# Sparse attention and mixture of experts on one core: q, k and v laid out beforehand, loaded into the tiles' own order

## The chip, the cores and the metric

The kernel runs on one core of one Trainium2 chip. The metric is the device time of one launch in microseconds, the median of several runs. A profile is one execution recorded by the hardware profiler; its span runs from the first to the last instruction. The arrays that a launch gets are prepared on the host by numpy; that is outside the time, in both kernels.

## The reference

Attention over q, k, v of shape (8 batches, 8 heads, 576 positions, 64), float32. Heads 0 to 3 see the last 32 positions (local), heads 4 to 7 the positions with the same remainder by 32 (strided). Its output, reshaped to 4608 tokens of 512, goes through a mixture of 8 experts, two for each token.

```python
scores = scale * np.matmul(q, k.transpose(0, 1, 3, 2))          # scale = 1/8
mask_local = (rel >= 0) & (rel < 32)                            # rel = pos[:, None] - pos[None, :]
mask_strided = (rel >= 0) & (pos[None, :] % 32 == pos[:, None] % 32)
scores = np.where(masks[None], scores, -1e9)
attn = np.exp(scores - scores.max(-1, keepdims=True))
attn = attn / (attn.sum(-1, keepdims=True) + 1e-09)
out = np.matmul(attn, v)
# then, for each token x of 512: the two best of 8 experts by x @ w_gate + softplus(x @ w_noise) * noise
out[token] += weight * (np.maximum(x @ w1[e], 0) @ w2[e])
```

## The kernel before

The work is written as pieces (`Piece`), each with an engine, an assumed duration, what it reads and writes, and a rank. A planner (`issue_all`, L296) walks through them with a clock of its own and writes them out in the order in which each engine could take them; pieces marked ANY go to ACT or DVE, whichever is free first. Buffers are rings (`Ring`): a piece that allocates the n-th slot waits for the users of the slot before it. When the planner sees PE waiting for an attention piece, it puts matmuls of zeros into the gap (L375, padding, one for each 150 ns that it reckons). Loads and stores are issued by SP, in order, on one queue; GpSimd issues the scatters and gathers, in order too. Zero stores to the output (12 of 0.79 MB) have the lowest rank and are taken when the planner's queue is nearly empty.

**Attention.** A unit is one batch, one pair of heads, local or strided: 32 units, four to a batch, strided first. For each unit:

- `loads` (L447): k and q as rows of positions (ks, qs or raw), v into v_s by way of vraw, or straight into v_l in pieces of 64 numbers, and v_0, the first 64 rows again.
- `prep` (L494): k and q are turned by PE, four groups of transposes a unit (L519 strided, four to a group; L515 local, three to a group, after a reordering copy into ord). ACT or DVE evacuates each group into kT or qT (q times the scale). For strided heads eight more small copies fill the ninth block. kT and qT have one buffer of each kind.
- `products` (L541): masks (L560) and scores (L567) into two PSUM banks, five blocks in each.
- `item` (L580), twice a unit, i = 0 and 1: maxima (L594), exps (L598, L600), transposes of the weights (L608) and their copies (aT), the value matmuls (L627, L632), row sums, reciprocals and scaling (L637 to L657) into xo. The value tiles hold a column of ones, so that the row sums come out of the same matmuls. The item with i = 1 has a fifth, extra block, whose two heads lie in the 64 lower partitions side by side in columns (`extra`).
- `finish` (L666): xo goes to x_dram by SP (L673), and is transposed for the gate (L694, L698).

After four units `route` (L723) runs the gate matmuls (L744) and, on ACT and DVE, picks two experts for each token; GpSimd scatters the entries into the experts' lists (L834). So there are eight gates, one a batch.

**Experts.** Six lists can be started before all batches are known: two are known after batches 2 and 3, the others later. Layer 1 is L1062, layer 2 is L1114; the weights are loaded in 160 pieces (wraw) and split in two parts by ACT and DVE (L904, L905). Results (res, a ring of four) are scatter-added to the output by GpSimd (L1150), after the zero stores of those rows.

Of the kernel before, what the change touches and what calls it, by code (L numbers as in the profile page):

```python
# [22 lines left out]
def kernel(  # L23
    ctx: ExitStack,
    tc: tile.TileContext,
    q: bass.AP,
    k: bass.AP,
    v: bass.AP,
# [8 lines left out]
    B, H, S, D = q.shape  # L37
# [5 lines left out]
    NP = HL // 2  # L43
    QB = 64
# [7 lines left out]
    LP, LJ = S // 6, 6  # L52
# [105 lines left out]
    kT_l = keep.tile([128, STRIDE + S], F32, name="kT_l")  # L158
    qT_l = keep.tile([128, NBL, QB], F32, name="qT_l")
    kT_s = keep.tile([128, NBL, G], F32, name="kT_s")  # L160
    qT_s = keep.tile([128, NBL, G], F32, name="qT_s")
    v_l = [keep.tile([KW, 2, NBL, D + 1], F32, name=f"v_l{i}") for i in range(2)]
    v_s = [keep.tile([G, 2, NJ, D + 1], F32, name=f"v_s{i}") for i in range(2)]

    v_0 = [keep.tile([G, 2, D + 1], F32, name=f"v_0{i}") for i in range(2)]
    xo_ = [keep.tile([128, 5, 2, D], F32, name=f"xo{i}") for i in range(3)]
    nc.vector.memset(kT_l[:, :STRIDE], 0.0)
    for i in range(2):
        nc.vector.memset(v_l[i][:, :, :, D:D + 1], 1.0)
        nc.vector.memset(v_l[i][:STRIDE, 0, 0, :], 0.0)  # L170
        nc.vector.memset(v_0[i][QB:], 0.0)
        nc.vector.memset(v_0[i][:QB, :, D:D + 1], 1.0)
        nc.vector.memset(v_s[i][:, :, :, D:D + 1], 1.0)
    nc.vector.memset(kT_s[:, NBL - 1, QB:], 0.0)
    for x in xo_:
        nc.vector.memset(x[QB:, 4, :, :], 0.0)
# [264 lines left out]
    R["v_l"], R["v_s"], R["v_0"] = Ring(2, fixed=v_l), Ring(2, fixed=v_s), Ring(2, fixed=v_0)  # L441

    def base_of(u):
        b, p, local = units[u]
        return (b * H + (2 * p if local else HL + 2 * p)) * S * D

    def loads(u, rank):  # L447

        base, local = base_of(u), units[u][2]
        res = {}  # L450

# [846 lines left out]
```

## Time and profile before

| what | us |
|---|---|
| median of 3 runs (1105.77 to 1109.4) | 1107.29 |
| the profiled execution | 1117.46 |
| its span | 1115.7 |
| fourth gate, where the first expert list follows | 151 |
| eighth and last gate | 366 |

The page gives each engine's busy time: PE runs matmuls, PEld loads their weights beside them, DVE and ACT are the vector engines, POOL is GpSimd, SP issues DMAs. The chain of work is followed back from the last instruction, at each step to what released it. A row `L515 x3` in the chain means three instructions of line 515 in a row, with the time that they held the chain. In rows by line, `145/161/164` are the shortest, median and longest duration in ns.

### The profile page before, as it was taken

The page shows a single profiled execution, that of the slowest core. Times are in us where ns is not written, and L with a number is a line of the kernel's source. Part 1 is how long each engine was busy: PE and PEld are TensorE (multiplying, and loading weights), DVE is VectorE, ACT ScalarE, POOL GpSimd, SP SyncE. Part 2 cuts the span into 40 slices and gives each one's busy share as a digit, 9 for nine tenths or more (in the row PEclk, how much of TensorE's full clock was granted, in tenths as well). Part 3 has the DMA queues.
Part 4 walks back from the last instruction along what each step waited for, and adds up shares of the span by engine and source line. Part 5 has one row for each costly group of instructions (what it writes and reads, how often), then busy time and mean ns, then how long its engine had stood idle before and what let it go on. Part 6 is the DMA issues. An engine that isn't in the chain of part 4 may idle for free.

```text
span 1115.7 us, 23537 instructions
## 1 busy us (share of the span) xinstructions
PE 1069.2 (96%) x8790; PEld 945.9 (85%) x8790; DVE 556.0 (50%) x1536; ACT 474.3 (43%) x1203; POOL 539.8 (48%) x661
## 2 busy tenths in 40 slices
PE   8988887989999999999999999999999999999997
PEld 7867766888788898988879898989989898989886
DVE  7857766865476224624746236323633462355231
ACT  6867766766565222423433224222512252244221
POOL 1044334423424467655668475646554655556432
PEclk9998989989999999999999999999999999999999
DMA  9986857878785134543555235523642363243222
GB/s 199 241 195 153 221 137 207 193 179 208 181 245 136 29 52 97 137 75 72 141 133 133 43 57 136 115 44 54 163 85 46 59 179 61 44 116 81 43 46 31
DMA packets 168430, 133.03 MB, mean 119 GB/s; under 512 B 51864, under 2 KB 136344, under 8 KB 168296
## 3 DMA queue, kind: packets, MB, share of 16 engines
q1 hardware_dynamic: 145160, 92.31, 32.1%
q0 software_dynamic: 23136, 38.94, 19.9%
q8 instruction: 83, 1.36, 0.5%
q14 instruction: 51, 0.42, 0.1%
HBM read 92.85 MB, written 39.39 MB: 119 GB/s over the span
## 4 chain that ended last, share of the span: by engine, by line
PE 87%; issue 5%; DVE 3%; DMA 1%; ACT 1%; POOL 1%; another core or an unknown queue 1%; POOLq 0%; SPq 0%; DVEq 0%; ACTq 0%
PE bankB L1114 6%; PE bankE L1114 5%; PE bankF L1114 5%; PE bankC L1062 5%; PE bankH L1062 5%; PE bankG L1062 5%; PE bankE L1062 5%; PE bankC L1114 5%; PE bankF L1062 4%; PE bankD L1062 4%; PE bankA L1062 4%; PE bankA L1114 4%; PE bankB L1062 4%; PE bankG L1114 4%; PE bankH L1114 3%
## 5 line engine op out<-in xcount | busy, mean ns | idle before, releaser
L985 POOL DMA_INDIRECT xg<-x_dram,gxx x248 | 258.5, 1043 | 165.8 <-DVE xr L1024 71.8
L1150 POOL DMA_INDIRECT out_dram<-res,tabt x80 | 133.4, 1667 | 99.7 <-ACT res L289 54.0
L834 POOL DMA_INDIRECT tab<-ent,addr x96 | 91.3, 951 | 89.9 <-issue 26.8
L1024 DVE STREAM_TRANSPOSE xr<-xg 128x512 f32<-128x512 f32 (+1 forms) x66 | 68.1, 1032 | 42.4 <-DMA xg<-x_dram,gxx 33.8
L1031 ACT CAST xhi<-xr 128x512 fp32r<-128x512 f32 (+1 forms) x66 | 39.1, 592 | 53.1 <-DVE xr L1024 51.2
L1033 DVE TENSOR_TENSOR xlo<-xr,xhi 128x512 fp32r<-128x512 f32 (+1 forms) x66 | 43.5, 659 | 35.9 <-ACT xhi L1031 25.2
L905 DVE TENSOR_TENSOR w1lo<-wraw,w1hi 128x512 fp32r<-128x512 f32 x80 | 54.5, 686 | 3.7 <-ACT w1hi L904 1.3
L905 DVE TENSOR_TENSOR w2lo<-wraw,w2hi 128x512 fp32r<-128x512 f32 x80 | 51.8, 684 | 1.2 <-ACT xT L288 0.7
L994 POOL TENSOR_SCALAR gix<-tabt 128x2 int32<-128x2 int32 (+1 forms) x32 | 8.0, 251 | 88.2 <-DMA tabt<-tab 71.0
L904 ACT CAST w1hi<-wraw 128x512 fp32r<-128x512 f32 x80 | 49.0, 618 | 0.4 <-DMA wraw<-in_moe_w_dram 0.2
L904 ACT CAST w2hi<-wraw 128x512 fp32r<-128x512 f32 x80 | 46.6, 617 | 3.3 <-DMA wraw<-in_moe_w_dram 2.7
L1062 PE MATMUL bankH<-xhi,w1hi 128*128 128x256 f32 (+3 forms) x132 | 40.5, 307 | 0.8 <-issue 0.8
L1062 PE MATMUL bankG<-xhi,w1hi 128*128 128x256 f32 (+3 forms) x132 | 40.0, 303 | 0.6 <-issue 0.6
L1062 PE MATMUL bankG<-xlo,w1hi 128*128 128x256 f32 (+3 forms) x132 | 39.4, 299 | 1.0 <-issue 1.0
L1062 PE MATMUL bankC<-xhi,w1hi 128*128 128x256 f32 (+3 forms) x132 | 39.8, 301 | 0.0
L1062 PE MATMUL bankH<-xhi,w1lo 128*128 128x256 f32 (+3 forms) x132 | 39.6, 300 | 0.0
L1062 PE MATMUL bankH<-xlo,w1hi 128*128 128x256 f32 (+3 forms) x132 | 39.6, 300 | 0.0
L1062 PE MATMUL bankG<-xhi,w1lo 128*128 128x256 f32 (+3 forms) x132 | 39.4, 298 | 0.0
L1062 PE MATMUL bankC<-xlo,w1hi 128*128 128x256 f32 (+3 forms) x132 | 39.1, 296 | 0.1
L1062 PE MATMUL bankC<-xhi,w1lo 128*128 128x256 f32 (+3 forms) x132 | 39.2, 297 | 0.0
L1114 PE MATMUL bankB<-w2hi,hhi 128*128 128x512 f32 x96 | 38.9, 405 | 0.0
L1062 PE MATMUL bankF<-xhi,w1hi 128*128 128x256 f32 (+3 forms) x128 | 38.2, 299 | 0.4 <-issue 0.4
(696 smaller groups left out, 3545.8 us busy)
## 6 DMA issues: line engine op xcount, KB each, us to landing
wraw<-in_moe_w_dram SPq DMA_DIRECT2D x160, 256.0 KB
out_dram<-zeros SPq DMA_DIRECT2D x12, 768.0 KB
ks<-in_k_dram SPq DMA_DIRECT2D x15, 320.0 KB
qs<-in_q_dram SPq DMA_DIRECT2D x15, 320.0 KB
vraw<-in_v_dram SPq DMA_DIRECT2D x30, 160.0 KB
raw<-in_k_dram SPq DMA_DIRECT2D x16, 288.0 KB
v_l<-in_v_dram SPq DMA_DIRECT2D x16, 288.0 KB
raw<-in_q_dram SPq DMA_DIRECT2D x16, 288.0 KB
```

The lines of the kernel that those rows point to most:

```text
L834: st = nc.gpsimd.indirect_dma_start(out=tab, out_offset=bass.IndirectOffsetOnAxis(ap=s["addr"].t[:, t, kk:kk + 1], axis=0), in_=s["ent"].t ...
L904: Piece("ACT", 620, lambda o: nc.scalar.copy(hi.t, raw.t), rank, read=[raw], alloc=[hi], expert=True)
L905: Piece("DVE", 715, lambda o: nc.vector.tensor_tensor(lo.t, raw.t, hi.t.bitcast(F32), ALU.subtract), rank, read=[raw, hi], alloc=[lo], exp ...
L985: dma(lambda o, g=g: nc.gpsimd.indirect_dma_start(out=xg.t[:, g, :], out_offset=None, in_=x_dram[:4 * known, :], in_offset=bass.IndirectOf ...
L994: nc.gpsimd.tensor_scalar(gi.t[:, :nb], tb.t[:, :nb, 0], known - 1, None, op0=ALU.min)
L1024: Piece("DVE", 8.8 * rows, lambda o, xg=xg, xr=xr, ng=ng, rows=rows: nc.vector.transpose(xr.t.rearrange("p (c x) -> p c x", c=ND)[:, :, :r ...
L1031: Piece("ACT", 620 * rows // 128, lambda o, view=view, cols=cols: nc.scalar.copy(xh.t[:, :, cols], view()), rank, read=[xr], expert=True, ...
L1033: Piece("DVE", 725 * rows // 128, lambda o, view=view, cols=cols: nc.vector.tensor_tensor(xl.t[:, :, cols], view(), xh.t[:, :, cols].bitca ...
L1062: nc.tensor.matmul(ps.t[:, :width], a.t[:, 128 * d:128 * d + 128], c.t[:, d, :width], start=(m == 0), stop=(m == len(todo) - 1))
L1114: nc.tensor.matmul(ps.t, HT[n, f][p[0]].t[:, cols], W2[n][f][p[1]].t, start=(m == 0), stop=(m == len(todo) - 1))
L1150: st = nc.gpsimd.indirect_dma_start(out=out[:known, :], out_offset=bass.IndirectOffsetOnAxis(ap=places(), axis=0), in_=y.t[:rows, :], in_o ...
```

## The change

The host turns q and k of each unit and stacks the two heads, so that a load fills kT and qT in place, 128 rows of 2304 or 2560 bytes. v is laid out with its column of ones; rows are 4680 bytes, and the strided tile holds the ninth block (the first 64 rows again) too. `prep` is gone with its transposes, evacuations and copies, and so are raw, ord, ks, qs, vraw and v_0. kT and qT get two buffers of each kind; mx goes from 3 to 5, ex and aT from 2 to 3, rs from 2 to 4 buffers, res from 4 to 3. q is no longer scaled: a tensor_scalar multiplies the maximum by the scale, and the exps apply it to the scores. The two heads of the extra block now lie one above the other in 128 partitions: one sum and one reciprocal cover all five blocks, and two copies with a factor, on ACT or DVE, take the extra blocks to xo in place of one product on DVE.

```diff
     R = {}
     for name, shape, dtype, depth in (
-            ("raw", [LP, 2, LJ, D], F32, 2), ("ord", [LP, LJ, 2, D], F32, 1),
-            ("vraw", [GP, NJ, D], F32, 1), ("ks", [GP, 2, NJ, D], F32, 1), ("qs", [GP, 2, NJ, D], F32, 1),
-            ("mx", [128, 5], F32, 3), ("ex", [128, 5, KW], F32, 2), ("aT", [128, 5, 128], F32, 2),
-            ("rs", [128, 6], F32, 2),
+            ("mx", [128, 5], F32, 5), ("ex", [128, 5, KW], F32, 3), ("aT", [128, 5, 128], F32, 3),
+            ("rs", [128, 6], F32, 4),
...
-    R["kT_l"], R["qT_l"] = Ring(1, fixed=[kT_l]), Ring(1, fixed=[qT_l])
-    R["kT_s"], R["qT_s"] = Ring(1, fixed=[kT_s]), Ring(1, fixed=[qT_s])
+    R["kT_l"], R["qT_l"] = Ring(2, fixed=kT_l), Ring(2, fixed=qT_l)
+    R["kT_s"], R["qT_s"] = Ring(2, fixed=kT_s), Ring(2, fixed=qT_s)
...
+        def put(key, ring, sel, src, rows, width, rank):
+            slot = res[key] = R[ring].new()
+            dma(lambda o: nc.sync.dma_start(sel(slot.t), dram(src, n * rows * width, [[width, rows], [1, width]])),
+                4 * rows * width, rank, alloc=[slot])
...
+            put("k", "kT_l", lambda t: t[:, STRIDE:], k_l, 128, S, rank)
+            put("q", "qT_l", lambda t: t.rearrange("r n x -> r (n x)"), q_l, 128, S, rank)
+            put("v", "v_l", lambda t: t[STRIDE:].rearrange("p h n d -> p (h n d)"), v_l, QB, VW, v_rank)
...
+            put("k", "kT_s", lambda t: t.rearrange("r n x -> r (n x)")[:, :8 * G + QB], k_s, 128, 8 * G + QB, rank)
+            put("q", "qT_s", lambda t: t.rearrange("r n x -> r (n x)"), q_s, 128, S, rank)
+            put("v", "v_s", lambda t: t.rearrange("p h n d -> p (h n d)"), v_s, GP, VW, v_rank)
         return res
-
-    def prep(u, L, rank):
...
+        Piece("DVE", 90, lambda o: nc.vector.tensor_scalar(mx.t, mx.t, scale, None, op0=ALU.mult), rank, write=[mx],
+              read=[mx])
+
         def exps(o):
             for n in range(4):
-                nc.scalar.activation(exv()[:, n, :], view(sc)[:, n, :], AF.Exp, bias=mx.t[:, n:n + 1])
+                nc.scalar.activation(exv()[:, n, :], view(sc)[:, n, :], AF.Exp, bias=mx.t[:, n:n + 1], scale=scale)
...
-                    rhs = L["v"].t[:, h, NBL - 1, :] if local else L["v0"].t[:, h, :]
-                    nc.tensor.matmul(extra()[:, h, :], aT.t[:w, 4, 64 * h:64 * h + 64], rhs, start=True, stop=True)
+                    rhs = L["v"].t[:w, h, NBL - 1, :]
+                    nc.tensor.matmul(main(5)[64 * h:64 * h + 64, 4, :], aT.t[:w, 4, 64 * h:64 * h + 64], rhs, start=True,
+                                     stop=True)
...
-            nc.vector.tensor_scalar(rs.t[:, :4], main()[:, :, D], 1e-9, None, op0=ALU.add)
-            if nb > 4:
-                nc.vector.tensor_scalar(rs.t[:QB, 4:], extra()[:, :, D], 1e-9, None, op0=ALU.add)
+            nc.vector.tensor_scalar(rs.t[:, :nb], main(nb)[:, :, D], 1e-9, None, op0=ALU.add)
...
-            if nb > 4:
-                nc.vector.tensor_tensor(xo.t[:QB, 4, :, :], extra()[:, :, :D],
-                                        rs.t[:QB, 4:, None].to_broadcast([QB, 2, D]), ALU.mult)
...
+        for h, r in enumerate(halves) if nb > 4 else ():
+            Piece("ANY", {"ACT": 270, "DVE": dve(D)}, lambda o, h=h, r=r: copy(
+                o.e, xo.t[:QB, 4, h, :], main(5)[r, 4, :D], rs.t[r, 4:5]), rank, read=[po, rs], write=[xo])
...
-            ("res", [128, DM], F32, 4)):
+            ("res", [128, DM], F32, 3)):
...
+def _laid_out(q, k, v):
...
+    def turned(a):
+        return a.transpose(0, 1, 2, 4, 3).reshape(B, NP, 2 * D, -1)
...
+    vl = np.ones((B, NP, QB, 2, NB, D + 1), v.dtype)
+    vl[..., :D] = pairs(v, 0).reshape(B, NP, 2, NB, QB, D).transpose(0, 1, 4, 2, 3, 5)
...
+    return {"q_l": turned(pairs(q, 0)), "k_l": turned(pairs(k, 0)), "v_l": vl,
+            "q_s": strided(q, G - QB), "k_s": strided(k, 0), "v_s": vs}
```

Because the planner sets the order, it moves as a whole. Three places matter.

PE at the start of the program, behind the warm-up (zeros), before: the four groups that turn k and q of the first strided unit, then its masks.

```order
L337 MATMUL bankH<-zeros 128x256
L519 MATMUL bankA<-ident,ks 128x72 x4
L519 MATMUL bankB<-ident,ks 128x72 x4
L519 MATMUL bankC<-ident,qs 128x72 x4
L519 MATMUL bankD<-ident,qs 128x72 x4
L560 LDWEIGHTS twin
L560 MATMUL bankE<-mask_s,twin 64x288
```

PE at the same place after the change:

```order
L331 MATMUL bankH<-zeros 128x256
L481 LDWEIGHTS twin
L481 MATMUL bankA<-mask_s,twin 64x288
L481 LDWEIGHTS twin
L481 MATMUL bankA<-mask_s,twin 64x72
```

The masks follow the warm-up at once. Over the whole program 448 transposes in 128 groups are gone, and the padding of zeros grows from 137 to 210 matmuls.

PE behind the fourth gate, where the first expert list begins, before: scores of the next local unit (L567), then a matmul of zeros (L1069) and layer 1 (L1062).

```order
L567 MATMUL bankB<-kT_l,qT_l 64x96
L567 MATMUL bankD<-kT_l,qT_l 64x96
L1069 LDWEIGHTS zeros
L1069 MATMUL bankE<-zeros 128x256
L1062 MATMUL bankE<-xhi,w1hi 128x256
```

And after, where padding is L369, values are L547 and L552, transposed weights L531, layer 1 L977:

```order
L369 LDWEIGHTS zeros
L369 MATMUL bankE<-zeros 128x256
L547 MATMUL bankE<-vt_s_147,aT 64x65 x8
L552 MATMUL bankE<-vt_s_147,aT 64x65 x2
L531 MATMUL bankB<-ident,ex 96x128 x4
L984 LDWEIGHTS zeros
L984 MATMUL bankC<-zeros 128x256
L977 MATMUL bankC<-xhi,w1hi 128x256
```

The first list moves further into the fifth batch. Ahead of the last gate stand 216 layer-1 and 120 layer-2 matmuls, where there were 372 and 168.

SP at the end of batch 2, before: the first zero store (L1199) stands between stores of xo (L673) and loads (L455).

```order
L455 DMA vraw<-in_v_dram 80x512
L673 DMA x_dram<-xo_147 128x2x128
L673 DMA x_dram<-xo_147 64x128
L1199 DMA out_dram<-zeros 1536x1x128
L455 DMA raw<-in_q_dram 96x2x384
L455 DMA v_l_140<-in_v_dram 64x18x64
```

SP after the change, around the last store of batch 7 (the rows of xo_148), where the first zero stores (L1114) now are:

```order
L1114 DMA out_dram<-zeros 1536x1x128
L443 DMA vt_l_145<-in_v_l_dram 64x1170
L1114 DMA out_dram<-zeros 1536x1x128
L588 DMA x_dram<-xo_148 128x4x128
L588 DMA x_dram<-xo_148 64x128
L1114 DMA out_dram<-zeros 1536x1x128 x2
L588 DMA x_dram<-xo_149 128x2x128 x2
```

All twelve zero stores move behind the loads of batch 7; SP issues 96 loads of q, k and v in place of 128.

More of the change, by code (lines that the diff above doesn't have):

```diff
@@ L25 @@
     tc: tile.TileContext,
-    q: bass.AP,
-    k: bass.AP,
-    v: bass.AP,
+    q_l: bass.AP,
+    k_l: bass.AP,
+    v_l: bass.AP,
+    q_s: bass.AP,
+    k_s: bass.AP,
+    v_s: bass.AP,
     w_gate: bass.AP,
@@ L156 @@
     psum = actx.enter_context(tc.tile_pool(name="psum", bufs=1, space=PSUM))
[L158 to L165, printed above, removed]
+    kT_l = [keep.tile([128, STRIDE + S], F32, name=f"kT_l{i}") for i in range(2)]
+    qT_l = [keep.tile([128, NBL, QB], F32, name=f"qT_l{i}") for i in range(2)]
+    kT_s = [keep.tile([128, NBL, G], F32, name=f"kT_s{i}") for i in range(2)]
+    qT_s = [keep.tile([128, NBL, QB], F32, name=f"qT_s{i}") for i in range(2)]
+    vt_l = [keep.tile([KW, 2, NBL, D + 1], F32, name=f"vt_l{i}") for i in range(2)]
+    vt_s = [keep.tile([GP, 2, NBL, D + 1], F32, name=f"vt_s{i}") for i in range(2)]
     xo_ = [keep.tile([128, 5, 2, D], F32, name=f"xo{i}") for i in range(3)]
-    nc.vector.memset(kT_l[:, :STRIDE], 0.0)
     for i in range(2):
[L169 to L176, printed above, removed]
+        nc.vector.memset(kT_l[i][:, :STRIDE], 0.0)
+        nc.vector.memset(kT_s[i][:, NBL - 1, QB:], 0.0)
+        nc.vector.memset(vt_l[i][:STRIDE, 0, 0, :], 0.0)
     nc.vector.memset(run, 0.0)
@@ L444, in base_of, with loads @@
+    def loads(u, rank, v_rank=None):
         b, p, local = units[u]
[L445 to L450, printed above, removed]
[L452 to L468 removed]
@@ L476, in front @@
             def front(o):
-                vv = slot.t.rearrange("p h n d -> p (h n) d")
-                copy(o.e, vv[:STRIDE, 1:, :D], vv[QB:, :2 * NBL - 1, :D])
-            Piece("ANY", {"ACT": act(64 * (2 * NBL - 1)), "DVE": 760}, front, rank, read=[slot], write=[slot])
-        else:
-            slot = res["v"] = R["v_s"].new()
-            for h in range(2):
-                put(f"v{h}raw", R["vraw"].new(), [(lambda t: t[:rows].rearrange("p j d -> p (j d)"), v, base + h * S * D,
-                                                   [[NJ * D, rows], [1, NJ * D]], 2048 * rows)], True)
-                def spread(o, h=h, raw=res[f"v{h}raw"]):
-                    copy(o.e, slot.t[:G, h, :, :D], raw.t[:G])
-                Piece("ANY", {"ACT": act(NJ * D), "DVE": 420}, spread, rank, read=[res[f"v{h}raw"]],
-                      **{"write" if h else "alloc": [slot]})
-            put("v0", R["v_0"].new(),
-                [(lambda t: t[:QB, :, :D], v, base, [[D, QB], [S * D, 2], [1, D]], 65536)], True)
@@ new lines, in front @@
+                vv = slot.t.rearrange("p h n d -> p (h n d)")
+                copy(o.e, vv[:STRIDE, D + 1:], vv[QB:, :VW - D - 1])
+            Piece("ANY", {"ACT": act(VW - D - 1), "DVE": 760}, front, rank, read=[slot], write=[slot])
+        else:
+            put("k", "kT_s", lambda t: t.rearrange("r n x -> r (n x)")[:, :8 * G + QB], k_s, 128, 8 * G + QB, rank)
+            put("q", "qT_s", lambda t: t.rearrange("r n x -> r (n x)"), q_s, 128, S, rank)
+            put("v", "v_s", lambda t: t.rearrange("p h n d -> p (h n d)"), v_s, GP, VW, v_rank)
@@ L565, in product @@
                 rhs = kT.t[r, QB * blk:QB * blk + KW] if local else kT.t[r, blk, :]
-                q0 = 0 if local or blk == NBL - 1 else G0
-                nc.tensor.matmul(sv[b][halves[half], s, :], qT.t[r, blk, q0:q0 + QB], rhs, start=False,
+                nc.tensor.matmul(sv[b][halves[half], s, :], qT.t[r, blk, :], rhs, start=False,
                                  stop=True, skip_group_check=True)
@@ L1286 @@
     arrays, args = {}, []
-    for name in _INS:
-        a = _np.ascontiguousarray(inputs[name])
+    given = _laid_out(inputs["q"], inputs["k"], inputs["v"])
+    given.update((name, inputs[name]) for name in _INS)
+    for name in given:
+        a = _np.ascontiguousarray(given[name])
         arrays[f"in_{name}_dram"] = a
```

117 lines of the change are left out of this document (35 added, 82 removed).

## The prediction

> **What bounds the kernel now.** I read the page first, for the engines and for the chain of work that ended last.
>
> ```profile
> span 1115.7 us, 23537 instructions
> PE 1069.2 (96%) x8790; PEld 945.9 (85%) x8790; DVE 556.0 (50%) x1536; ACT 474.3 (43%) x1203; POOL 539.8 (48%) x661
> PE 87%; issue 5%; DVE 3%; DMA 1%; ACT 1%; POOL 1%; another core or an unknown queue 1%; POOLq 0%; SPq 0%; DVEq 0%; ACTq 0%
> ```
>
> TensorE (PE) is busy for 96% of the span and carries 87% of the chain. That is an average over stages, so I then cut the span at the gate matmuls. The timeline shows them for the fourth and for the last batch:
>
> ```profile
> 151.25 2.78 PE L744 MATMUL bankF<-xT,wg 128*32 128x192 f32 x24
> ...
> 365.60 1.50 PE L744 MATMUL bankD<-xT,wg 128*32 128x192 f32 x24
> ```
>
> The busy time by stretch, from two answers of the same view (columns: stretch, length, PE, PEld, DVE, ACT, POOL, granted clock, DMA share, GB/s):
>
> ```profile
> 0.00:152.00 152.00, 132.94 (x2092) 108.61 (x2095) 109.92 (x449) 109.11 (x350) 44.42 (x113) 0.97 0.84 196
> 25.00:50.00 25.00, 24.60 (x454) 20.93 (x453) 21.43 (x78) 21.95 (x79) 0.00 (x0) 1.00 0.93 234
> ...
> 152.00:366.00 214.00, 200.18 (x2321) 172.35 (x2318) 136.54 (x488) 136.25 (x384) 79.15 (x131) 0.97 0.74 186
> ```
> ```profile
> 79.00:114.00 35.00, 31.41 (x466) 26.18 (x463) 25.31 (x108) 27.07 (x89) 12.51 (x27) 0.90 0.75 166
> ...
> 366.00:1116.00 750.00, 736.08 (x4389) 664.91 (x4383) 309.53 (x599) 228.94 (x471) 416.22 (x418) 0.99 0.40 85
> ```
>
> There are three stages. To 152 us there is attention alone: PE, DVE, ACT and the DMA engines are all well filled (87%, 72%, 72%, 84%), and part of what PE does there is padding. From 152 to 366 us attention and the first expert lists share PE, which idles 13.8 of 214 us. After 366 us the experts alone keep PE busy for 736 of 750 us, and nothing there is edited. So what the change brings is how much earlier the last gate comes, corrected for expert work that moves across it.
>
> **What the change removes.** The transposes of q and k (L515, L519), first to 152 us, then to 366 us, and the padding matmuls (L375), which all lie before 152 us:
>
> ```profile
> 0.00:152.00 152.00, 15.72 (x108) 10.61 (x108) 0.97 0.84 196
> 152.00:366.00 214.00, 11.96 (x84) 9.37 (x84) 0.97 0.74 186
> ```
> ```profile
> 0.00:152.00 152.00, 15.15 (x152) 13.08 (x152) 0.97 0.84 196
> 152.00:366.00 214.00, 10.40 (x104) 9.16 (x104) 0.97 0.74 186
> ```
> ```profile
> 0.00:152.00 152.00, 20.21 (x137) 13.28 (x137) 0.97 0.84 196
> ```
>
> Their busy time, 53.2 us, overlaps other matmuls. What a group holds PE for is seen in the chain (start, length):
>
> ```profile
> 22.25 0.47 PE bankA L515 x3
> 22.71 0.25 PE bankC L515 x3
> ...
> 25.14 0.25 PE bankB L519 x4
> ...
> 27.68 0.11 PE bankG L375
> ```
>
> 0.25 us a group packed, up to 0.47 us with its wait. On ACT and DVE go the evacuations, the reordering copies (ord) and the spreads (v_s). By tile over the whole run, columns PE, PEld, DVE, ACT; the PE figures are mostly other work:
>
> ```profile
> 0.00:1116.00 1116.00, 17.71 (x576) 13.93 (x576) 10.89 (x40) 16.66 (x57) 0.99 0.53 119
> ```
> ```profile
> 0.00:1116.00 1116.00, 17.71 (x576) 13.93 (x576) 11.51 (x43) 16.21 (x53) 0.99 0.53 119
> ```
> ```profile
> 0.00:1116.00 1116.00, 19.29 (x576) 17.91 (x576) 6.92 (x16) 7.84 (x17) 0.99 0.53 119
> ```
> ```profile
> 0.00:1116.00 1116.00, 19.29 (x576) 17.91 (x576) 8.21 (x18) 6.69 (x14) 0.99 0.53 119
> ```
> ```profile
> 0.00:1116.00 1116.00, 27.67 (x192) 19.98 (x192) 5.48 (x10) 18.29 (x22) 0.99 0.53 119
> ```
> ```profile
> 0.00:1116.00 1116.00, 24.06 (x512) 19.32 (x512) 6.84 (x18) 9.86 (x16) 0.99 0.53 119
> ```
>
> These are kT_s, qT_s, kT_l, qT_l, ord and v_s: 49.9 us on DVE and 75.6 us on ACT, 125 of the 492 us that the two do before 366 us. They bound nothing by themselves there (64 to 72% busy), so I book no time of their own for them; they let PE's waits shrink.
>
> **What it adds.** The extra blocks' own sums, reciprocal and scaling go; two copies of 64x64 and a scaling of mx (128x5) come. Nearest rows:
>
> ```profile
> L639 DVE TENSOR_SCALAR rs<-bankG x7: 141/142/145, 24.2 to 345.2; 64x2 f32<-64x2 f32 x7
> ```
> ```profile
> L644 DVE RECIPROCAL rs<-rs x32: 124/126/128, 18.3 to 359.1; 64x2 f32<-64x2 f32 x32
> ```
> ```profile
> L656 DVE TENSOR_TENSOR xo<-bankG,rs x7: 268/273/273, 24.9 to 345.8; 64x128 f32<-64x128 f32 x7
> ```
> ```profile
> L288 ACT COPY xT<-bankA x5: 212/212/234, 43.2 to 218.4; 128x64 f32<-128x64 f32 x5
> ```
>
> Gone: 32 x (142 + 126 + 273) = 17.3 us of DVE. New: 64 x 0.21 = 13.4 us on either engine, and 64 scalings that no row shows: between 0.06 us (half of L644, the smallest DVE row here) and 0.14 us (L639), 4 to 9 us; I take 0.13. All of it is covered by the 125 us removed. The scaling also stands between the maximum and the exps; three ex and five mx buffers cover that, and without the cover it is 64 x 0.13 = 8 us. The scale inside the exps is free: the same 320 instructions. Two of the new copies in place of one product change nothing on PE, which has the same 64 extra value matmuls.
>
> Padding rises from 137 to 210 matmuls, 73 x 0.11 = 8 us. It fills waits of PE and costs nothing as long as they last; if they are gone, 8 us. That the order holds more of it says that PE is expected to wait, not to be full, before the first list.
>
> res has three buffers for four. The next block comes 5.4 us later (second row below); a scatter takes 1.67 us behind its write, so three slots last 16 us. Cost nothing in the last stage.
>
> ```profile
> L1150 POOL DMA_INDIRECT out_dram<-res,tabt x80 | 133.4, 1667 | 99.7 <-ACT res L289 54.0
> ```
> ```profile
> 464.35 2.10 PE bankB L1062 x12
> ...
> 530.35 5.45 PE bankE L1114 x24
> ```
>
> The zero stores move behind batch 7's stores. The first scatter to the output needs three of them (2.4 MB, 12 us at 196 GB/s); on GpSimd batch 7's table scatters queue behind it, and on ACT the fourth res write and the exps behind that. If SP is late, up to 12 us; I take none, since PE holds four unfinished lists there.
>
> **The sum, first stage.** PE without the transposes and the padding would need 132.9 - 15.7 - 15.2 - 20.2 = 82 us; DVE and ACT about 75 us each (219 less 58% of 121, the share of the transposes that falls here). The DMA engines need more: counted from SP's order, 27.4 MB are issued up to the fourth batch's last store (28.9 before), and with the 1 MB of other traffic that the run had on top (29.8 MB at 196 GB/s), 28.4 MB. At the 234 GB/s of 25 to 50 us that is 121 us, at the stage's 196 GB/s 145 us. The loads now have two sets of buffers and no step behind them, so the queue is filled more evenly; I take the middle, 215 GB/s: 132 us, a gain of 20 (7 to 31).
>
> One row bears on the wide rows that the change brings (256-byte packets of v are gone). From 12 to 18 us most packets were small ones:
>
> ```profile
> DMA packets 2375, 1.36 MB, mean 226 GB/s; under 512 B 1782, under 2 KB 2153, under 8 KB 2373
> ```
>
> 226 GB/s, 3% under the best stretch, so I book nothing for packet size. The Trainium skill (DMA: Bandwidth & Descriptors, Specifications) has it that a transfer needs 512 bytes to run at line rate. By that rule the 5.8 MB of v in such pieces (16 x 0.29 and 16 x 0.066, 10 of 16 loads in this stage) cost about double, an estimate of 17 us more gain in this stage and 11 in the next, a sum of 1041 us; this row does not bear it out.
>
> **Second stage.** 84/3 + 104/4 = 54 groups go. Packed they are 54 x 0.25 = 13.5 us, by busy time 22.4; I take 18, since the chain shows both kinds. DMA needs 33 MB in it, 177 us at 186 GB/s, and 214 - 18 - 34 (below) = 162 us asks for 204 GB/s, between the two rates.
>
> **Expert work that moves.** By the order, 216 instead of 372 layer-1 and 120 instead of 168 layer-2 matmuls stand before the last gate. 84 of the former are 384 wide (2.10 us for 12), 72 are 256 wide, two thirds of that, 48 are L1114: 14.7 + 8.4 + 10.9 = 34 us less before the gate and 34 more behind it, where PE is full. Net 0. So the last gate should come at 366 - 20 - 18 - 34 = 294 us, and 784 us should follow.
>
> The profiled execution took 1117.5 us (span 1115.7); the sum is -20 - 18 = -38 us. The runs without profile have their median at 1107.3, 10 us lower, and the same work in them, so I forecast **1069 us**; its own range is 1053 (both terms at their best) to 1085 (-10 and -13).
>
> **Rivals.**
> *The DMA engines keep their pace.* If loads, not copies, set the rate, stage one takes 28.4 MB / 196 = 145 us (-7) and stage two 33 / 186 = 177, against 180 without it (-3): 1097 us. For it: share 0.84, and 0.93 while PE was fullest. Against: ACT and DVE rows stand between load and product today. Chance 0.15.
> *All waits go.* 234 GB/s throughout (-31), and stage two loses its 22 us of transposes and its 14 us idle: -67, 1040 us. Against: four engines with hand-overs have never been that tight here. 0.14.
> *Wide rows move slower (slower).* v now comes in 64 or 80 rows of 4680 bytes, few pieces for 16 engines, and products wait for whole tiles. Both stages hold 28.4 + 33 = 61.4 MB; the last gate must come by 332 us (366 - 34) to break even, so it decides at 185 GB/s, hardly below the 190 of today. At 170 GB/s the gate comes at 361 us, +29: 1136 us. For it, a v_l load on the chain:
>
> ```profile
> 8.87 8.71 DMA v_l<-in_v_dram
> ```
>
> 8.7 us for 0.29 MB, but beside other loads. Against: every filled stretch above ran at 196 GB/s or more. 0.08.
> *PE's clock falls.* With more waiting the granted clock of stage one could drop; it was 0.90 in 79 to 114 us with PE 90% busy. At half clock PE's 82 us become 164: +12, less 18, 1101 us. The Trainium skill (TensorE: Matmul & The Clock Gate, HAM oscillation) states that idle gaps over some 3.4 us halve the clock; that speaks against taking work off a waiting PE, and the padding is there to meet it. 0.05.
> That the change does not do what it says is out: the order has no q or k transposes left.
>
> **How the numbers follow.** 0.58 for the forecast, 0.15 + 0.14 + 0.08 + 0.05 for the rivals. The range runs from 1042 (most of the way to "all waits go") to 1097 (the DMA pace) and leaves out slower and the tail, under 0.2. This kernel's runs tell 0.3%, 3.3 us, from no change. Faster: 0.58 + 0.15 + 0.14 and part of the clock's case, 0.89; same 0.03; slower 0.08.
>
> **What would show it.** After: no transposes of q and k; the fourth gate near 132 us and the last near 294; DMA over 200 GB/s to there; PE full behind it with 784 us to go; mx scaling near 0.13 us. The forecast is wrong if the last gate comes after 320 us, if PE waits for loads at 196 GB/s or less, if ACT waits at a res write around batch 7, or if PE idles more than 20 us after the last gate.

## The result, and the profile after

| | before | after | ratio, 95% interval |
|---|---|---|---|
| first set of runs, median (us) | 1106.53 (1105.01 to 1109.4, 4 runs) | 1079.1 (1073.75 to 1082.25, 4 runs) | 0.974 (0.970 to 0.979) |
| the profiled executions (us) | 1117.46 | 1080.45 | |
| a later set on another chip, median (us) | 1110.07 (1105.52 to 1114.21, 7 runs) | 1073.69 (1069.96 to 1079.05, 4 runs) | 0.969 (0.963 to 0.974) |

The kernel became faster by 27 us in the first set and by 36 us in the second. The forecast was 1069 us with a range of 1042 to 1097. Against the profiled execution, on which the sum was made, the difference is 37 us, for 38 in the sum.

The page of the kernel after, first lines and the chain:

```profile
span 1078.2 us, 22402 instructions
PE 1043.4 (97%) x8415; PEld 916.9 (85%) x8415; DVE 516.0 (48%) x1373; ACT 424.1 (39%) x1069; POOL 538.2 (50%) x661
PE 90%; issue 5%; DMA 1%; DVE 1%; ACT 1%; POOL 1%; SPq 0%; POOLq 0%; another core or an unknown queue 0%; DVEq 0%; ACTq 0%
```

PE lost 26 us of busy time, DVE 40 and ACT 50. The fourth and the last gate in the timeline (start, length):

```profile
133.65 1.50 PE L659 MATMUL bankE<-xT,wg 128*32 128x192 f32 x24
...
295.03 1.50 PE L659 MATMUL bankH<-xT,wg 128*32 128x192 f32 x24
```

They stood at 151.25 and 365.60; 132 and 294 were forecast. The three stages, in the columns of before (stretch, length, PE, PEld, DVE, ACT, POOL, clock, DMA share, GB/s):

```profile
0.00:134.00 134.00, 119.41 (x1903) 93.51 (x1906) 85.96 (x357) 86.10 (x279) 43.59 (x109) 0.94 0.79 211
134.00:295.00 161.00, 154.00 (x1910) 125.22 (x1901) 101.43 (x387) 92.44 (x288) 64.53 (x123) 0.96 0.75 194
295.00:1079.00 784.00, 769.99 (x4609) 698.16 (x4608) 328.64 (x632) 245.54 (x503) 430.08 (x431) 0.99 0.44 94
```

DVE and ACT are now busy for 64% of the first stage, not 72%; the last stage is as full as before. The last gate came 71 us earlier, but expert work was moved across it. Expert matmuls that still stand before it, layer 1 (L977) and layer 2 (L1029):

```profile
0.00:295.00 295.00, 37.10 (x216) 32.24 (x216) 0.95 0.77 202
```
```profile
0.00:295.00 295.00, 34.01 (x120) 21.99 (x120) 0.95 0.77 202
```

That is 71.1 us, for 63.89 + 45.97 = 109.9 before. **Last gate less the expert work ahead of it** takes that move out: 365.6 - 109.9 = 255.7 us before, 295.0 - 71.1 = 223.9 us after. I call it the attention's time; it fell by 32 us. It still counts TensorE's waits, and expert matmuls fill some of them, so it compares only kernels with much expert work ahead of the last gate. One run below has hardly any (6.5 us), and there it says little. For every run, each with its own rows read in the same way:

| kernel | ratio to before (95%) | fourth gate | last gate | expert PE ahead | attention's time |
|---|---|---|---|---|---|
| before | | 151.3 | 365.6 | 109.9 | 255.7 |
| before, again | 1.005 (1.002 to 1.009) | 152.4 | 366.7 | 111.9 | 254.8 |
| after | 0.974 (0.970 to 0.979) | 133.7 | 295.0 | 71.1 | 223.9 |
| after, again | 0.969 (0.963 to 0.974) | 131.2 | 290.5 | 68.9 | 221.6 |
| after, no padding | 0.976 (0.972 to 0.980) | 140.0 | 299.2 | 70.5 | 228.7 |
| after, half the loads | 0.968 (0.964 to 0.973) | 131.0 | 294.0 | 70.4 | 223.5 |
| after, both of these | 0.975 (0.970 to 0.979) | 136.0 | 295.2 | 69.0 | 226.2 |
| after, single tiles | 0.980 (0.975 to 0.985) | 153.2 | 345.0 | 105.9 | 239.1 |
| after, transposes back | 0.987 (0.983 to 0.991) | 139.3 | 308.7 | 69.1 | 239.6 |
| after, copies back | 1.014 (1.009 to 1.019) | 151.3 | 316.6 | 61.9 | 254.6 |
| after, copies planned | 1.006 (1.004 to 1.008) | 140.5 | 273.8 | 6.5 | 267.3 |
| after, v in pieces | 0.973 (0.968 to 0.978) | 136.0 | 295.3 | 68.5 | 226.8 |
| after, no scaling of mx | 0.962 (0.960 to 0.964) | 133.0 | 293.4 | 71.3 | 222.1 |
| before, deeper | 1.003 (0.999 to 1.006) | 143.9 | 338.8 | 85.0 | 253.7 |

Two profiles of one kernel agree in it within 2.3 us.

### The profile page after: what moved, and what is told of

Read it like the earlier page. It is cut to its first block, busy times and chain, and to the rows that moved or that the text cites. A ratio compares the mean times of both kernels' runs of the same rounds, so it can differ in the third digit from the quotient of the medians.

```text
span 1078.2 us, 22402 instructions
## 1 busy us (share of the span) xinstructions
PE 1043.4 (97%) x8415; PEld 916.9 (85%) x8415; DVE 516.0 (48%) x1373; ACT 424.1 (39%) x1069; POOL 538.2 (50%) x661
## 4 chain that ended last, share of the span: by engine, by line
PE 90%; issue 5%; DMA 1%; DVE 1%; ACT 1%; POOL 1%; SPq 0%; POOLq 0%; another core or an unknown queue 0%; DVEq 0%; ACTq 0%
PE bankB L1029 5%; PE bankE L1029 5%; PE bankD L1029 5%; PE bankC L977 5%; PE bankH L977 5%; PE bankF L977 5%; PE bankC L1029 5%; PE bankB L977 5%; PE bankA L977 4%; PE bankE L977 4%; PE bankG L977 4%; PE bankA L1029 4%; PE bankF L1029 4%; PE bankD L977 4%; PE bankH L1029 4%
## 5 line engine op out<-in xcount | busy, mean ns | idle before, releaser
L1065 POOL DMA_INDIRECT out_dram<-res,tabt x80 | 130.7, 1634 | 85.9 <-ACT res L283 53.8
L749 POOL DMA_INDIRECT tab<-ent,addr x96 | 93.8, 977 | 90.7 <-issue 17.5
L977 PE MATMUL bankC<-xhi,w1lo 128*128 128x256 f32 (+3 forms) x136 | 40.3, 296 | 1.0 <-issue 1.0
L977 PE MATMUL bankC<-xhi,w1hi 128*128 128x256 f32 (+3 forms) x136 | 40.8, 300 | 0.2 <-issue 0.2
L977 PE MATMUL bankC<-xlo,w1hi 128*128 128x256 f32 (+3 forms) x136 | 40.3, 297 | 0.5 <-issue 0.5
L977 PE MATMUL bankH<-xhi,w1hi 128*128 128x256 f32 (+3 forms) x132 | 39.9, 302 | 0.3 <-issue 0.3
L977 PE MATMUL bankF<-xhi,w1hi 128*128 128x256 f32 (+3 forms) x132 | 39.6, 300 | 0.2 <-issue 0.2
L977 PE MATMUL bankH<-xlo,w1hi 128*128 128x256 f32 (+3 forms) x132 | 39.1, 296 | 0.8 <-issue 0.8
L977 PE MATMUL bankF<-xlo,w1hi 128*128 128x256 f32 (+3 forms) x132 | 39.2, 297 | 0.5 <-issue 0.4
L977 PE MATMUL bankF<-xhi,w1lo 128*128 128x256 f32 (+3 forms) x132 | 39.2, 297 | 0.0
L977 PE MATMUL bankH<-xhi,w1lo 128*128 128x256 f32 (+3 forms) x132 | 39.2, 297 | 0.0
L977 PE MATMUL bankA<-xhi,w1hi 128*128 128x256 f32 (+3 forms) x128 | 38.3, 299 | 0.0
L977 PE MATMUL bankA<-xhi,w1lo 128*128 128x256 f32 (+3 forms) x128 | 37.8, 296 | 0.0
## 6 DMA issues: line engine op xcount, KB each, us to landing
vt_s<-in_v_s_dram SPq DMA_DIRECT2D x16, 365.6 KB
```

Source lines behind the costliest of these rows:

```text
L749: st = nc.gpsimd.indirect_dma_start(out=tab, out_offset=bass.IndirectOffsetOnAxis(ap=s["addr"].t[:, t, kk:kk + 1], axis=0), in_=s["ent"].t ...
L977: nc.tensor.matmul(ps.t[:, :width], a.t[:, 128 * d:128 * d + 128], c.t[:, d, :width], start=(m == 0), stop=(m == len(todo) - 1))
L1065: st = nc.gpsimd.indirect_dma_start(out=out[:known, :], out_offset=bass.IndirectOffsetOnAxis(ap=places(), axis=0), in_=y.t[:rows, :], in_o ...
```

## The experiments

The theory behind the first stage's term was that the DMA engines set the time to the fourth gate (28.4 MB at 215 GB/s). Its rivals: TensorE's own work does, or the hand-overs between TensorE, DVE and ACT.

**The kernels, unedited.** No edit; both were run once more.

> The kernel before, unedited, run and profiled a second time. The miss of the forecast (1069 against 1079.1 us measured) is the 10 us by which before's profiled execution (1117.5) was longer than its median (1106.5). Theory A: that execution was an outlier, and the change is worth 1106.5 - 1079.1 = 27 us in any pair of typical executions; the second profile is then at 1104 to 1110 us, with the 10 us missing before the last gate (365.6 us in the first profile, 355 to 360 in this one), where the chip's clock and the loads vary. Rival B: the profiled kernel is slower than the unprofiled one by 10 us each time (the profile's cost), and this one is again at 1115 to 1119 us with the last gate at 363 to 368. The kernel after was profiled at 1080.5 with a median of 1079.1, which speaks for A. Ratio to before: 1.000 within 0.3%.

1120.2 us (1111.3 to 1127.5, 10 runs) beside 1114.3 us (17 runs of the same kernel on that chip). The profile has B's numbers (span 1118.3, last gate 366.7), but not its cause: the runs without a profile were as long here, and the second profile of after, below, was shorter than its median. The runs do show that one kernel beside itself gave a ratio of 1.005 (1.002 to 1.009), so the 0.3% that the prediction took for the measurement's limit is too fine; under 0.5% I read nothing. Within these ten runs the time goes with the mean granted clock: 1111.29 us at 0.985, 1125.95 at 0.973.

> The kernel after, unedited, beside the kernel before on the same chip, as the mark for the other runs here: the ratio 0.974 again, within 0.005 (two sets of runs of one kernel differed by 0.5% in e1_before_again), and the last gate at 293 to 297 us. If the profiled executions of before were 1117 and 1118 us by chance, this one may stand up to 8 us over its first profile; if the change is worth 38 us, as the sum had it, the ratio is 0.966.

0.969, with a span of 1067.8 us in the profile. The fourth and the last gate:

```profile
131.20 1.50 PE L659 MATMUL bankE<-xT,wg 128*32 128x192 f32 x24
...
290.51 1.50 PE L659 MATMUL bankH<-xT,wg 128*32 128x192 f32 x24
```

The ratio is at the edge of what was expected, and the last gate came before the 293 to 297 us expected. So the change is worth 27 to 36 us. The forecast's 38 is just outside; of the 10 us by which it missed the first median, the second set of the same kernel takes away 5.

**Padding and loads**, a table of two by two.

```diff
-                for i in range(int((room - 150) // 150)):
+                for i in range(0):
```
```diff
-            dma(lambda o: nc.sync.dma_start(sel(slot.t), dram(src, n * rows * width, [[width, rows], [1, width]])),
+            part = width if u < 4 else width // 2
+            dma(lambda o: nc.sync.dma_start(sel(slot.t)[:, :part],
+                                            dram(src, n * rows * width, [[width, rows], [1, part]])),
```

> The kernel after without the 210 padding matmuls (33 us of PE's busy time, 28 of them before the fourth gate). Theory A (the padding lies in waits of PE and keeps its clock up; the waits are set by loads and hand-overs): the same time within 3 us, 1077 to 1082, or slower if the clock falls: fourth gate at 131 to 140 us, PE waits of 40 us in place of 14, granted clock of the stage below 0.94. Rival B (the padding is longer than the wait it stands in, as its rows on the chain of the kernel after suggest: 1.42 us before a value group, 1.31, 1.28): the fourth gate comes 8 to 20 us earlier, at 114 to 126 us, and the whole takes 1059 to 1071 us.

> The kernel after with the loads of q, k and v of all but the first four units cut to half their columns (the rest of each tile keeps what an earlier load left there, so those results are not the reference's). About 6 MB of the 28.3 MB of the first stage go, and 6 to 7 of the 31.3 MB of the second; the instructions on PE, DVE and ACT are the same. Theory A (the loads set the pace of the first stage, as the prediction's 28.4 MB at 215 GB/s had it): 22 MB at 211 GB/s are 105 us, so PE with its padding, 119 us busy, becomes the bound: fourth gate at 119 to 124 us, the last at 272 to 285, total 1055 to 1070. Rival B (PE's own order with padding and hand-overs sets it): the gate stays at 130 to 134 us, the last at 290 to 295, total 1074 to 1080. If PE's waits with no releaser ('issue', 0.5 us in front of each score matmul L487) come from full DMA queues, they shrink here from about 6 us in the stage to below 3.

> The kernel after with both edits: half the columns of q, k and v loaded from the fifth unit on (those results are not the reference's) and no padding matmuls. With e2_no_padding and e3_half_loads it makes a table of two by two. Theory A (loads set the pace): PE's 91 us without padding and 22 MB at 211 GB/s, 105 us, put the fourth gate at 105 to 112 us, clearly ahead of either edit alone, total 1045 to 1060. Rival B (hand-overs between PE, DVE and ACT): no more than without the padding alone, within 3 us of that run.

From the start to the last gate: after as it is, without padding, with half the loads, with both (columns as above).

```profile
0.00:295.00 295.00, 273.42 (x3807) 218.72 (x3807) 187.39 (x742) 178.54 (x566) 108.12 (x231) 0.95 0.77 202
```
```profile
0.00:299.20 299.20, 265.13 (x3597) 210.87 (x3597) 187.13 (x742) 178.03 (x566) 108.17 (x231) 0.87 0.77 199
```
```profile
0.00:294.00 294.00, 269.25 (x3810) 215.34 (x3813) 187.28 (x742) 178.86 (x566) 109.13 (x231) 0.97 0.65 158
```
```profile
0.00:295.00 295.00, 260.04 (x3597) 206.22 (x3597) 187.38 (x742) 177.75 (x566) 107.53 (x231) 0.90 0.62 157
```

Read the last two columns first. With half the loads DMA falls from 202 to 158 GB/s and its share from 0.77 to 0.65, while the gates stay where they were (131.0 and 294.0, for 131.2 to 133.7 and 290.5 to 295.0). **The loads do not set the pace;** the rate follows the pace. The first stage's term of the prediction rested on the opposite. Without padding, half the loads brought the fourth gate 4 us forward (136.0 for 140.0), little more than the 2.5 us by which the two profiles of after differ there.

Then PE and its clock. The padding was 33 us of PE's busy time (210 matmuls):

```profile
0.00:295.00 295.00, 33.03 (x210) 20.19 (x210) 0.95 0.77 202
```

Without it PE is busy for only 8 us less. Part of the 33 us overlaps other matmuls: counted from the trace, those others kept PE busy for 251 of the 273 us, and for 265 without padding, 14 us more. The granted clock goes from 0.95 to 0.87. In the first stage it fell furthest, from 0.93 to 0.76 (after, then without padding, and three of the waits without padding):

```profile
5.00:134.00 129.00, 115.54 (x1886) 90.73 (x1887) 84.32 (x349) 84.82 (x278) 40.87 (x94) 0.93 0.80 212
```
```profile
5.00:134.00 129.00, 106.44 (x1631) 81.48 (x1629) 80.95 (x337) 79.97 (x262) 37.55 (x88) 0.76 0.80 202
```
```profile
PE bankA L613 <- DVE xo L567: 2.3, 2, 1.4
PE bankD L710 <- DVE ohs L701: 2.2, 1, 2.2
...
PE bankC L531 <- ACT ex L521: 1.5, 1, 1.5
```

With the padding gone the waits lie open (total, times, longest). They come to 21.9 us, not the 40 expected: 9.7 on DVE (above all for xo, the attention's output, and ohs, of the gate), 6.4 on ACT, 5.8 with no releaser, none on a load. This fits the rival, hand-overs between the engines.

The fourth gate comes 6 to 9 us later and the attention's time grows by 5 to 7 us; with the loads halved in both it is 5 and 3 us, and 0.7% in the whole (0.975 for 0.968, with intervals that overlap). So the padding is no work that could be saved: it holds the clock up. That the whole kernel is slower without it isn't clear of the scatter. The Trainium skill (TensorE: Matmul & The Clock Gate, HAM oscillation) has idle gaps of more than some 3.4 us bring the clock down; the direction agrees, but the longest single wait of PE in this stretch is the 2.2 us of the second row, so here many shorter ones went with it.

The waits of PE without a releaser ahead of the score matmuls, 6.4 us from 5 to 134 us of after, were 3.8 us with half the loads: neither below the 3 us expected nor unchanged. Whether full DMA queues cause them stays open.

**v in small pieces.**

```diff
+            dims = [[D + 1, rows], [rows * (D + 1), 2 * NBL], [1, D + 1]] if key == "v" else [[width, rows], [1, width]]
...
+    vl, vs = (y.transpose(0, 1, 3, 4, 2, 5) for y in (vl, vs))
```

> The kernel after with v laid out in memory so that each row comes in 18 pieces of 260 bytes in place of one of 4680; all else is the same. 10.5 MB of v in all, 5 of them before the fourth gate. The prediction booked nothing for the size of packets. Theory A (by the row of before in which small packets moved at 226 GB/s, and by the halved loads, which brought 1 us): no change, 0.965 to 0.975 of before, gates at 130 to 134 and 289 to 296. Rival B (small pieces cost double): 5 MB more in each stage at 211 GB/s, 24 us a stage if loads set the pace; since halving them did not show that, 24 us less the waits they have room in, some 5 to 15 us more in the whole, ratio 0.975 to 0.985. By the Trainium skill (DMA: Bandwidth & Descriptors, Specifications), which asks for 512 bytes a transfer, it should be B.

0.973, between the two sets of the kernel after: no change that can be told. The last gate lies in the range of theory A; the fourth, at 136.0 us, is 2 us past it. DMA packets in 0 to 134 us, after and with pieces:

```profile
DMA packets 28151, 28.25 MB, mean 211 GB/s; under 512 B 6511, under 2 KB 20810, under 8 KB 28129
```
```profile
DMA packets 49170, 27.76 MB, mean 207 GB/s; under 512 B 29732, under 2 KB 43132, under 8 KB 49148
```
```profile
0.00:134.00 134.00, 116.88 (x1875) 91.64 (x1876) 84.27 (x351) 84.29 (x275) 42.73 (x107) 0.94 0.88 207
```

The share rises from 0.79 to 0.88, 12 us of all 16 engines' time, for 21,000 packets more. Packet by packet in the traces, 23,328 packets of 260 bytes (6.1 MB) took 37.8 us of the 16 engines; the 1303 rows of 4680 bytes that they replace had taken 23.7. That is 1.6 times as much. The Trainium skill's rule on 512 bytes (DMA: Bandwidth & Descriptors, Specifications) is thus borne out in the engines' time. The 226 GB/s on which the prediction doubted it was too coarse a row: in 12 to 18 us of before the 1152 packets of 256 bytes are half of the packets, but 0.29 of 1.36 MB. It is not seen in the kernel's time, because loads are not what is waited for.

**TensorE's transposes back.** As many as were removed, results unread, the order otherwise that of after.

```diff
+            m, nt = (96, 12) if local else (72, 16)
+            for j in range(nt):
+                nc.tensor.transpose(sc[j % 2].t[:, :m], kT.t[:m, 128:256] if local else
+                                    kT.t[:m].rearrange("r n x -> r (n x)")[:, 128:256], ident[:m, :m])
```

> The kernel after with TensorE's share of the old work put back and nothing else: ahead of each score product 12 (local) or 16 (strided) transposes whose results are not used, 448 in all, 224 before the fourth gate; by the rows of before some 0.06 to 0.08 us each where packed, 1.0 us a unit, 32 us in all, 16 in each stage. The order is otherwise the same, padding too. Theory A (TensorE sets the pace to the last gate, since halved loads moved that gate by 1 us only): fourth gate at 147 to 152 us, last at 322 to 330, total 1105 to 1115 us, the whole gain gone. Rival B (hand-overs with DVE and ACT set it, and TensorE's work fits into waits): gate at 134 to 141, last at 295 to 308, total below 1092.

```profile
139.29 1.50 PE L663 MATMUL bankE<-xT,wg 128*32 128x192 f32 x24
...
308.72 1.50 PE L663 MATMUL bankH<-xT,wg 128*32 128x192 f32 x24
```
```profile
0.00:139.00 139.00, 21.31 (x252) 19.94 (x252) 0.98 0.79 206
139.00:308.00 169.00, 16.44 (x196) 15.42 (x196) 0.98 0.70 181
```

Against the kernel after on the same chip (131.2 and 290.5): 8 us by the fourth gate, 18 by the last, 22 in the whole. Between the theories: of 21.3 us of transposes in the first stage 8 show, of 16.4 in the second 10; the rest overlaps other matmuls or fits into waits.

**The load on DVE and ACT back**, nine copies a unit that nobody reads. First put into after's order, then known to the planner (the lower line in place of the upper).

```diff
...
+        for j in range(9):
+            def idle(o, u=u, t=LL[u]["k"], j=j):
+                src = t.t if units[u][2] else t.t.rearrange("r n x -> r (n x)")
+                return copy(o.e, spare[o.e], src[:, 32 * j:32 * j + 288])
+            Piece("DVE" if j % 2 else "ACT", 1, idle, rank - 2, read=[LL[u]["k"]])
```
```diff
+            Piece("ANY", {"ACT": act(288), "DVE": dve(288)}, idle, rank - 2, read=[LL[u]["k"]])
```

> The kernel after with the load on DVE and ACT put back and nothing else: for each unit four copies of 128x288 on DVE and five on ACT into tiles that nobody reads, by the rows of before 0.46 and 0.40 us each, 58 us on DVE and 64 on ACT in all. The order on TensorE is the same. Theory A (TensorE sets the pace; DVE and ACT are 65% busy and have room): total within 6 us of the kernel after, last gate before 300 us. Rival B (hand-overs set the pace): each unit is held 1 us, fourth gate at 142 to 152, last at 312 to 325, total 1096 to 1110 us.

1124.0 us beside 1073.7: 50 us more, beyond even what the rival had. In the profile 33 of them are the attention's time. The other 17 lie behind the last gate, where TensorE idles for 20 us in place of 9 and its matmuls take some 6 us longer (clock of the execution 0.979 for 0.992). The order did shift a little: 192 and 96 expert matmuls stand ahead of the last gate, for 216 and 120. The longest waits of TensorE for an aT, from 5 to 295 us (total, times, longest):

```profile
PE bankC L548 <- ACT aT L283: 2.1, 1, 2.1
PE bankE L548 <- ACT aT L283: 2.0, 1, 2.0
PE bankG L548 <- ACT aT L283: 1.9, 1, 1.9
```

Each wait is about as long as five copies in a row (5 x 0.43 = 2.2 us), and the trace has five or more of them on ACT just ahead of each of these three (once with another copy between): an aT stood behind a bunch. All waits for ACT there come to 24.6 us, for 2.2 in the kernel after. That could be the order's fault alone, so the planner got to know them:

> As the run with nine unread copies a unit (four on DVE, five on ACT), but the planner knows their length and chooses the engine, as it did for the copies of before; it plans a new order and adds some 180 padding matmuls. That run took 50 us more than the kernel after, twice the 1 us a unit that was expected. Theory A (DVE and ACT set the pace: they carry 219 us of work in the first stage of before and 173 in that of after): planned copies cost nearly as much, fourth gate at 143 to 155, last at 305 to 320, total 1095 to 1120 us, ratio 0.985 to 1.01. Rival B (those copies only stood at a bad place, five in a row ahead of an aT that TensorE waited for): planned ones fit in the free 35%, gate at 131 to 140, last below 302, ratio 0.968 to 0.98.

1116.5 us, 1.006 of before: the whole gain is gone with TensorE rid of its transposes and the loads as in after. The total is what theory A had, the gates are what rival B had. The first stage and the last gate:

```profile
5.00:141.00 136.00, 118.42 (x1927) 89.72 (x1928) 91.39 (x394) 115.50 (x368) 37.84 (x90) 0.97 0.78 208
```
```profile
140.46 1.50 PE L660 MATMUL bankE<-xT,wg 128*32 128x192 f32 x24
...
273.80 1.50 PE L660 MATMUL bankC<-xT,wg 128*32 128x192 f32 x24
```

The last gate comes earlier than in any other run, and yet the kernel is slow: the planner moved nearly all expert work behind it (6.5 us is left ahead). The attention's time, 267.3 us, is 46 more than after, but this is not the price of the copies. In the second stage TensorE now has waits that expert matmuls had filled, and padding takes their place, to the last gate 385 matmuls, 57 us, for 210 and 33 us in after:

```profile
0.00:273.80 273.80, 57.39 (x385) 35.80 (x385) 0.98 0.75 198
```

The second stage less its expert work is 127 us here and 90 in after; the first stage of after, which has no expert work and no copies, takes 131 for as many batches. So only the first stage is a fair comparison: 140.5 for 131.2 us, 9 us more. Why the planner chose that order stays open.

ACT was busy for 115.5 of 136 us, 85%; before had it at 72%. The planner took a copy on DVE for 457 ns and one on ACT for 378, and gave ACT two of three; they took some 305 and 432 (ns, min/median/max):

```profile
L283 ACT COPY spare_ACT<-kT_l x111: 414/432/454, 12.7 to 252.5; 128x288 f32<-128x288 f32 x111
```
```profile
L286 DVE COPY spare_DVE<-kT_s x62: 269/308/491, 5.9 to 247.2; 128x288 f32<-128x288 f32 x62
```

The run thus loads ACT harder than the old kernel did. That such copies cost time is shown, by the 9 us of its first stage; how much of the 32 us they were is not, nor that ACT is the engine that set the pace: of the 17.0 us that TensorE waited from 5 to 141 us, the trace puts 9.8 on DVE and 2.4 on ACT.

**Depth and second tiles.** Once taken away from after, once given to before.

```diff
-            ("mx", [128, 5], F32, 5), ("ex", [128, 5, KW], F32, 3), ("aT", [128, 5, 128], F32, 3),
-            ("rs", [128, 6], F32, 4),
+            ("mx", [128, 5], F32, 3), ("ex", [128, 5, KW], F32, 2), ("aT", [128, 5, 128], F32, 2),
+            ("rs", [128, 6], F32, 2),
...
-    R["kT_l"], R["qT_l"] = Ring(2, fixed=kT_l), Ring(2, fixed=qT_l)
+    R["kT_l"], R["qT_l"] = Ring(1, fixed=kT_l[:1]), Ring(1, fixed=qT_l[:1])
...
```

> The kernel after with one tile each for k and q of a kind in place of two, and the depths of before for mx, ex, aT and rs (3, 2, 2, 2); the order is planned anew for them, with 104 more padding matmuls. Theory A (the gain is PE's transposes; loads and depths were only there to let it show): within 8 us of the kernel after. Rival B (the second set of tiles and the depths bring most of the first stage's gain, since a product no longer waits for a load that could not start): the fourth gate falls back to 145 to 152 us and the last to 310 to 320, 1095 to 1105 us.

> The kernel before with the deeper buffers alone: mx 5 for 3, ex 3 for 2, rs 4 for 2 (aT stays at 2, and res goes to 3: there is no room for more). With the run that took them and the second k and q tiles away from the kernel after (1089.8 against 1073.7, 16 us) it shows where depth pays. Theory A (depth is a gain of its own): 8 to 16 us faster, ratio 0.985 to 0.993. Rival B (depth pays only once k and q come in two sets without a step of PE and an evacuation behind each load): within 4 us of before, ratio 0.996 to 1.004.

Last gates, after with single tiles and before with depth:

```profile
345.03 1.50 PE L659 MATMUL bankA<-xT,wg 128*32 128x192 f32 x24
```
```profile
338.76 1.50 PE L744 MATMUL bankD<-xT,wg 128*32 128x192 f32 x24
```

Less the expert work ahead of them, 239.1 and 253.7 us. So single tiles and shallow buffers cost after 17.5 us (16 in the whole, 0.980 for 0.969). That is short of the rival's 21 to 31 us and twice theory A's 8. All of it is in the first stage: the fourth gate comes at 153.2 us, no earlier than in before (151.3), with TensorE rid of its transposes. Deeper buffers bring before nothing in the whole: 253.7 for 255.7 in the profile, 1.003 (0.999 to 1.006) in the runs, as its rival B expected, although the fourth gate came 7 us earlier (143.9). Depth and second tiles together pay once the layout has taken the steps behind each load away. They were not taken apart, and the second run had aT at 2 and single k and q tiles, so those two weren't tried in before.

**The scaling of the maximum.**

```diff
-        Piece("DVE", 90, lambda o: nc.vector.tensor_scalar(mx.t, mx.t, scale, None, op0=ALU.mult), rank, write=[mx],
+        Piece("DVE", 90, lambda o: None, rank, write=[mx],
```

> The kernel after without the 64 scalings of the maximum (so the exps subtract the unscaled maximum: the results are not the reference's; the order is the same). Its rows took 0.16 us in the middle, and ACT waited for it 14 times, 19.5 us in all. Theory A (covered: ACT has slack, and the wait named is that of the reduction before it): within 3 us, ratio 0.966 to 0.972. Rival B (a step between the maximum and the exps that nothing covers): 64 x 0.16 = 10 us, half of it before the fourth gate, gates at 126 and 281, ratio 0.960.

In after this step took (second profile), and was waited for:

```profile
L516 DVE TENSOR_SCALAR mx<-mx x64: 127/162/292, 7.4 to 273.5; 128x5 f32<-128x5 f32 x64
...
  ACT ex L521: 19.5, 14
```

Without it 0.962 (0.960 to 0.964), for 0.969 (0.963 to 0.974) with it. The intervals overlap, and the gates didn't move (133.0 us for the fourth, and 293.4 less 71.3 is 222.1, for 221.6 to 223.9): some 5 us or none, not settled. The ACT waits that the view puts to it are at least not worth their 19.5 us.

## Why the prediction was right, step by step

**The sum.** First stage 152 to 132 forecast, 133.65 and 131.2 measured. Second stage 162 us long forecast, 161.4 and 159.3 measured. 784 us behind the last gate forecast, 783.2 measured in the first profile and 777.3 in the second. Expert work moved: 34 us forecast, 109.9 - 71.1 = 39 measured.

**The first stage's reason was wrong.** The step that failed is "The DMA engines need more", with "At the 234 GB/s of 25 to 50 us that is 121 us, at the stage's 196 GB/s 145 us". The share of 0.84 was read as a bound. Half the loads at 160 GB/s left the gate at 131 us. That the middle of that range, 215, met the measured 211 GB/s was luck: a pace set elsewhere happened to ask for it.

**What the first stage was made of.** Up to the fourth gate, counted from the traces' instructions (us):

| kernel | TensorE's matmuls without padding | its waits and padding | fourth gate |
|---|---|---|---|
| before | 121.1 | 30.1 | 151.3 |
| after | 100.4 | 33.2 | 133.7 |
| after, again | 98.5 | 32.7 | 131.2 |
| after, transposes back | 112.0 | 27.3 | 139.3 |
| after, copies planned | 98.0 | 42.4 | 140.5 |
| after, copies back | 103.5 | 47.8 | 151.3 |
| after, single tiles | 102.1 | 51.1 | 153.2 |

The prediction had it that DVE's and ACT's lost work would "let PE's waits shrink". Waits and padding did not shrink, they grew by 3 us, and the gain is about what TensorE lost of its own work. But that work is not the whole cause: put back alone, the transposes (13.5 of these 21 to 23 us of work) cost 8 of the 20 us and take the place of waits for the rest, and with single tiles their removal turns into waits altogether.

**The step "They bound nothing by themselves there ..., so I book no time of their own for them" failed too.** Copies on DVE and ACT alone, put back, cost 9 us of the first stage when planned and 20 when not, TensorE's transposes alone 8, single tiles and shallow buffers 22. Together that is far more than the 18 to 20 us of the change there, so they aren't shares of it. The order of each engine is fixed, and the runs fit a chain of hand-overs in which any of the three engines, given more to do, holds the others. Which part of the gain each removal brought by itself stays open.

**Second stage.** The length of 162 us came out because two errors cancelled: without the expert work that moved, the stage became 14 us shorter, not 18 (214.3 - 161.4 = 53, less 39), and 39 us of expert work moved, not 34. TensorE's transposes alone, put back, made it 10 us longer (169.4 for 159.3). Those were busy for 16.4 us, the old ones for 22.4, so the other 4 may be theirs too; no run shows it.

**Padding.** "costs nothing as long as they last" was right, and too modest: without it the fourth gate comes 5 to 9 us later. The rival on the clock named a mechanism that the run without padding shows. In after it came about only a little, because the padding grew with the waits: the clock of the first stage is 0.94 in the first profile and 0.97 in the second, for 0.97 before, and 0.77 without padding.

**Smaller steps.** The mx scaling took 0.16 us, not 0.13, and the two new copies to xo 0.31 us each on ACT, not 0.21. Wide rows didn't move slower. res at three buffers and the late zero stores show nothing: TensorE idles 13 of 783 us behind the last gate, as it did before (14 of 750).

**The forecast itself.** 38 us off the median gave 1069; the medians after were 1079.1 and 1073.7. The step that missed is the last one: the two profiled executions differ by 37 us, but the sets of runs by 27 and 36, and such sets scatter by half a per cent.

## What to carry to other kernels

A DMA share of 0.8 is no bound until fewer bytes make the kernel faster; and a PE that is padded through its waits looks like the bound on the chain, while 28 of its 119 busy us in the first stage are padding and it waits for DVE and ACT, which are 64% busy. Work taken from the busiest engine can turn into waits if the buffers don't let the next unit start: that is what single tiles did here. Where a planner moves work across a mark, compare the mark less that work, and check that the waits which that work filled haven't stayed behind. Steps that numpy does once outside the measured time (here the transposing of q and k) are a real gain in device time only if the inputs can come in that layout.

## What the runs showed of the hardware

- Leaving out 33 us of matmuls that computed nothing made TensorE busy for only 8 us less up to the last gate: the granted clock went from 0.95 to 0.87, and to 0.76 from 5 to 134 us, where no idle stretch of TensorE was longer than 2.2 us.
- 260-byte packets took 1.6 times the DMA engines' time of the same bytes in 4680-byte rows (37.8 us of 16 engines for 23.7), with no change of the kernel's time that could be told at a share of 0.88.
- Executions of one kernel on one chip spread by 1.4% (1111.3 to 1127.5 us), with mean granted clocks between 0.973 and 0.985.
